# Attention and expert layer on one core: from the tenth turn on, the sums of values and the fifth score chunk in one block

## The chip, the cores and the metric

The kernel runs on one core of one Trainium2 chip. The metric is the time of one execution on the device in microseconds (us), the median of repeated runs. The core has five engines that run side by side, each through its own instructions in a fixed order: TensorE (PE in the profile; its weight loads are PEld), VectorE (DVE), ScalarE (ACT), GpSimd (POOL) and SyncE (SP), which issues the DMAs.

## The reference

Block-causal attention over 8 batches and 8 heads (576 positions, head size 64, blocks of 64), then a two-layer expert network over the 4608 tokens of 512 features, without its bias or routing:

```python
scores = scale * np.matmul(q, k.transpose(0, 1, 3, 2))
mask = block_i >= block_j                      # blocks of 64
scores = np.where(mask, scores, -1000000000.0)
scores = scores - np.max(scores, axis=-1, keepdims=True)
attn = np.exp(scores)
attn = attn / (np.sum(attn, axis=-1, keepdims=True) + 1e-09)
attn = np.matmul(attn, v)
...
h = x @ w_in                                   # 512 -> 2048
g = h * (1.0 / (1.0 + np.exp(-1.702 * h)))
out = g @ w_out                                # 2048 -> 512
```

## The kernel before

**Two pieces of work share the core.** Attention goes in 32 turns n = 0 to 31, one for each pair of heads, and a 33rd that only finishes the last pair. The expert network goes in 12 tiles of 384 tokens, each in 16 slices of 128 hidden features. One slice has 12 products into the PSUM tile `hp` (x and w_in, each split in a high and a low part) and, a slice later, 9 products into three `acc` tiles (g and w_out, split in the same way). `hp` has one buffer. Between the two lies the nonlinearity: ACT computes a tanh from `hp` (L562), DVE makes g from it and `hp` (L563), ACT rounds g to `gh` (L571) and GpSimd computes the rest, `gl` (L82). So the products of slice k+1 into `hp` can't begin before DVE has made g of slice k, and `acc` of slice k comes behind `hp` of slice k+1.

**A turn of attention.** The queries of a head are cut in five chunks, i = 0 to 4; chunk i sees 64(2i+1) keys, so chunk 4 sees all 576. `prep` turns q and k with DVE transposes (L297) into `qk`, the two heads on partitions 0 to 63 and 64 to 127. `score` multiplies, each head on its half of TensorE's rows, so the two heads' products run side by side; a PSUM bank has room for 512 columns, so chunk 4 is cut in 256 and 320 keys and takes four banks. `weigh` masks, scales and takes the maximum on DVE (L351) and the exponential on ACT (L358). `normalise` divides (L368, L371 on DVE) and scales the weights, which `SCALE_ON` gives to an engine: "P" is GpSimd (L376), "D" is DVE (L378). `turn` transposes the weights in 32x32 blocks on DVE (L385, L390; called `turned` in the profile), and behind chunk 4 sixteen DMAs on SP's queue (L397) put these blocks in their places. `av` multiplies them with the values in the next turn, 60 products into two banks, and ACT copies the sums out (L450, L451).

**What sets the order.** `ORDER` writes out the items of a turn: from the tenth turn on (n = 9, since n = 8 has its own string) the third string holds, "3+0/2+1" (the scores of chunks 3, 0, 2, 1), "V" (sums of values of the pair before), "4" (chunk 4), "L" (transposes of the next pair). Between two items `advance` lays expert slices up to a quota from `TILES_BY`, in whole slices. The Tile framework then orders each engine's instructions; code under `high_priority` (the nonlinearity) may move ahead. `bank()` hands out four PSUM banks in rotation in these turns.

Of the kernel before, what the change touches and what calls it, by code (L numbers as in the profile page):

```python
# [10 lines left out]
F32 = mybir.dt.float32  # L11
# [5 lines left out]

SCALE_ON = ("PPPPP", "PPPPP", "PPPPD")  # L20

# [4 lines left out]
ORDER = (  # L26
# [3 lines left out]
)  # L30

START = "1+0 - B 2/3 L C - V - 4 - a - - -"
# [8 lines left out]
def attention_moe_kernel(  # L41
# [9 lines left out]
    nc = tc.nc  # L51
    B, H, S, D = q.shape
    DM, DF = w_in.shape
    P = 128
    BLK = 64
    NDC = DM // P
    NFC = DF // P
    RING = 2 * S
    TT = 384
    TILES = [(t0, min(TT, B * S - t0)) for t0 in range(0, B * S, TT)]  # L60
    NT = len(TILES)
    QC = 4
    NPAIR = B * H // 2
    HP = H // 2
    NCH = 5

    sp = ctx.enter_context(tc.tile_pool(name="sp", bufs=1))
# [6 lines left out]
    def early(n):  # L74

        return n < 2 * HP
# [12 lines left out]
    def bank():  # L89
        tags = ["w0", "w1", "w2"]  # L90
        if not turns["experts"]:
            tags += ["acc0", "acc1", "acc2", "h"]
        elif turns["n"] > 2 * HP:
            tags.append("w3")
        turns["bank"] += 1
        return ps.tile([P, 512], F32, tag=tags[turns["bank"] % len(tags)], name="bank")

    def mm(**kw):
        return tc.keep_in_program_order(nc.tensor.matmul(**kw))  # L99
# [4 lines left out]

    ident = sp.tile([P, P], F32, name="ident")
    make_identity(nc, ident)
    MW = 448
    mask = sp.tile([P, MW], mybir.dt.bfloat16, name="mask")
    nc.gpsimd.memset(mask, 0.0)
    nc.gpsimd.memset(mask[0:BLK, MW - BLK : MW], -8e9)  # L110

# [7 lines left out]
    def room(tag, shape, dt, name):  # L119
        return d2.tile(shape, dt, tag=tag, name=name, bufs=1)  # L120
# [6 lines left out]
        return home[name, g]  # L127

    xr = sp.tile([P, NDC, RING], F32, name="xr")


    vp = sp.tile([P, 2, NCH, D], F32, name="vp")
# [3 lines left out]
    def values(n):  # L136

        if n not in (1, 3):
            return vp
        if n not in vx:  # L140
            vx[n] = room("xl", [P, 2, NCH, D], F32, "vx")
            nc.gpsimd.memset(vx[n][BLK:P, :, NCH - 1, :], 0.0)
        return vx[n]
# [9 lines left out]
    tw, pw = [  # L153
        turned[:, x : x + 4 * NS].rearrange("p (b s) h c -> p b s h c", b=4) for x in (0, 4 * NS - 4)
    ]
# [5 lines left out]
    for i in range(NCH):  # L161
        w, o = BLK * (2 * i + 1), 2 * BLK * i * i
        es.append(flat[:, o : o + 2 * w].rearrange("p (h k) -> p h k", h=2))

    def width(i):
        return BLK * (2 * i + 1)

    def qrange(i):
        return (0, BLK) if i == 0 else (BLK * (2 * i - 1), BLK * (2 * i + 1))
# [6 lines left out]
    for g in range(NG):  # L176
# [3 lines left out]
        for fc in range(FG):  # L180
            r = (g * FG + fc) * P
# [80 lines left out]
    raw, qk = {}, {}  # L262
# [5 lines left out]
    def load(n):  # L268

        if n in (1, 3):  # L270
            raw[n] = room("xh", [P, 2, S // 32, 32], F32, "raw")
        else:
            raw[n] = d2.tile([P, 2, S // 32, 32], F32, tag="raw", name="raw", bufs=1)
        for x, src in enumerate((q, k)):
            queue = nc.scalar if n < 2 and x else nc.sync
            for hd, b, h in heads(n):
                for c in range(0, D, 32):
                    r = hd * D + c
                    queue.dma_start(
                        out=raw[n][r : r + 32, x],  # L280
                        in_=src[b, h][:, c : c + 32].rearrange("(c p) d -> p c d", p=32),
                    )
# [9 lines left out]
    def prep(n):  # L292

        tag = "e0" if early(n) and n % 2 else "qk"
        qk[n] = d2.tile([P, 2, S], F32, tag=tag, name="qk", bufs=1)
        for x in range(2):
            nc.vector.transpose(out=qk[n][:, x], in_=raw[n][:, x].rearrange("p c d -> p (c d)"))  # L297
        raw.pop(n)
        m = follower(n)
        if m is not None:  # L300
            load(m)

    stats = {}

    def score(n, banks):

        if n not in stats:
            mx = d2.tile([P, NCH + 1, 2], F32, tag="mx", name="mx")
            sm = d2.tile([P, NCH, 2], F32, tag="sm", name="sm")
            stats[n] = (mx, sm)  # L310
        todo = []
        for chunks in banks:

            part = []
            for lo, hi in ((0, 512),) if width(chunks[0]) <= 512 else ((0, 256), (256, S)):
                ss = [bank() for _ in range(2)]
                c = 0
                for i in chunks:
                    a, z = qrange(i)
                    w = min(hi, width(i)) - lo  # L320
                    for hd in range(2):
                        r = slice(hd * D, hd * D + D)

                        mm(
                            out=ss[hd][:, c : c + w], lhsT=qk[n][r, 0, a : a + P],
                            rhs=qk[n][r, 1, lo : lo + w], start=True, stop=True,
                        )
                        part.append((i, hd, lo, lo + w, ss[hd][0 : z - a, c : c + w]))
                    c += w
            todo.append(sorted(part, key=lambda x: (chunks[::-1].index(x[0]), x[2])))  # L330
        for chunks, part in zip(banks, todo):
            e = {}
            for i, hd, lo, hi, s in part:
                e[i] = weigh(n, i, hd, lo, hi, s, e.get(i))
            for i in chunks[::-1]:
                normalise(n, i, e[i])
                if not early(n):
                    turn(n, i, e[i])

    def weigh(n, i, hd, lo, hi, s, e):  # L340
# [8 lines left out]
        last = i > 0 and hi == w  # L349
        mk = mask[0:m, MW - (hi - lo) : MW] if last else mask[0:m, 0 : hi - lo]  # L350
        nc.vector.tensor_tensor_reduce(  # L351
# [12 lines left out]
    def normalise(n, i, e):  # L364
# [6 lines left out]
        nc.vector.reciprocal(out=c, in_=c)  # L371
        on = SCALE_ON[phase(n)][i]
        for hd in range(2):
# [52 lines left out]
                in_=src[:, x : x + 2 * len(part), a : a + 2],  # L426
            )

    def av(n):

        b, h = divmod(n, HP)
        before_av(n)
        o, o0 = bank(), bank()

        todo = []
        for i in range(1, NCH):
            c = (i - 1) * P
            todo += [(o, c, P, j, pw[:, :, SLOT[i] + j]) for j in range(i)]
            todo.append((o, c + BLK, BLK, i, pw[:, 2:4, 9 + i]))
        last = len(todo) - 1  # L440
        todo.append((o0, 0, BLK, 0, pw[:, 0:2, 10]))

        for x, (bk, c, nn, j, w) in enumerate(todo):
            for hd in range(2):
                mm(
                    out=bk[hd * D : hd * D + D, c : c + nn].rearrange("d (a c) -> d a c", c=32),
                    lhsT=values(n)[:, hd, j], rhs=w[:, :, hd], start=x in (0, last + 1), stop=x >= last,
                )
        c0 = (b % 2) * S
        nc.scalar.copy(out=xr[:, h, c0 : c0 + BLK], in_=o0[:, 0:BLK])  # L450
        nc.scalar.copy(out=xr[:, h, c0 + BLK : c0 + S], in_=o)  # L451
        m = follower(n)
        if m is not None:
            load_v(m)

    def follower(n):

        m = {0: 2, 1: 3, 2: 4, 3: None}.get(n, n + 1)
        return None if m is None or m >= NPAIR else m

    def order(n):
        return {HP: START, 2 * HP: HANDOVER}.get(n, ORDER[phase(n)]).split()

    def step(n):

        turns["n"] = n
        now = n < NPAIR

        def item(x):
            if x == "V":  # L470
                return (lambda: av(n - 1)) if n else None
            if x == "L":
                return (lambda: prep(n + 1)) if n + 1 < NPAIR else None
            if x in ("a", "B", "C"):
                m, chunks = {"a": (n, [0, 1]), "B": (n - 1, [2, 3]), "C": (n - 1, [4])}[x]
                return (lambda: flip(m, chunks)) if m >= 0 else None
            return (lambda: score(n, [[int(z) for z in y.split("+")] for y in x.split("/")])) if now and x != "-" else None

        return [item(x) for x in order(n)]
# [3 lines left out]
    xs = {}  # L483
# [22 lines left out]
    def chunk_time(tt):  # L506
        return 4 * unit1(tt) + tt // P * 650
# [69 lines left out]
        yield from second(prev)  # L577


    ends = np.cumsum([0.0] + [NFC * chunk_time(tt) for _, tt in TILES])  # L580

    def quota(pos):
        xs, ys = zip(*TILES_BY)
        return -1.0 if pos < xs[0] else np.interp(pos, xs, [ends[y if y >= 0 else y - 1] for y in ys])

    def heads_for(t):
        return -(-sum(TILES[t]) // S) * H
# [36 lines left out]
    for n in range(NPAIR + 1):  # L624
        items = step(n)
        for sl, fn in enumerate(items):
            if fn is not None:
                fn()
            if order(n)[sl] == "V":
                heads_done = 2 * n  # L630
            pos = 2 * (n + (sl + 1) / len(items))
            convert(min(len(pieces), np.interp(pos - 0.5, *zip(*WEIGHTS_BY))))
            lim = quota(pos)
            advance(heads_done, lambda: state["t"] >= lim)
# [30 lines left out]
```

## Time and profile before

| | |
|---|---|
| median of 3 runs (lowest to highest) | 1122.7 us (1121.84 to 1124.51) |
| the profiled execution | 1120.49 us, its span 1118.6 us |
| PE busy | 1076.4 us, 96% of the span |
| PEld busy | 908.7 us, 81% |
| DVE busy | 583.0 us, 52% |
| ACT busy | 498.6 us, 45% |
| POOL busy | 406.7 us, 36% |
| mean granted TensorE clock | 0.992 |

Busy time is the time in which an engine runs at least one instruction; matmuls are pipelined, so consecutive ones overlap in the list and only the distance of their starts tells their cost. "x60" stands for merged instructions of one kind. In the PE rows, "bank" with 60 instructions is the item V, with 16 the item 3+0/2+1, with 8 chunk 4; "hp" with 12 and "acc" with 9 are one slice's halves. A product in full float32 is two matmuls in the profile.

### The profile page before, as it was taken

How to read it: one execution, taken by the hardware profiler on the slowest of the kernel's cores; microseconds unless marked ns; L12 is line 12 of the kernel's file. 1: busy time of each engine (PE TensorE's matmuls, PEld its weight loads, DVE VectorE, ACT ScalarE, POOL GpSimd, SP SyncE). 2: the span in 40 equal slices, each digit the busy share in tenths (PEclk: the TensorE clock that was granted, in tenths of full speed). 3: DMA queues.
4: the chain of work that ended last, by engine and by line, in shares of the span. 5: the costliest groups of instructions: out<-in, count | busy, mean ns of one | idle time of the engine just before them, and what ended most of it. 6: DMA issues, size and time to landing. Idle time of an engine off the chain costs nothing. (4 is left out here: it accounts for less than half of the span.)

```text
span 1118.6 us, 19977 instructions
## 1 busy us (share of the span) xinstructions
PE 1076.4 (96%) x6960; PEld 908.7 (81%) x6960; DVE 583.0 (52%) x1856; ACT 498.6 (45%) x1321; POOL 406.7 (36%) x509
## 2 busy tenths in 40 slices
PE   5969998999999999999999999999999999999998
PEld 3757776788888888888888888888888888899997
DVE  6776885545545555654555655645545654211210
ACT  5866776434534433534443543444434444322322
POOL 4665664333333332333333333333333233122222
PEclk9979999999999999999999999999999999999999
DMA  8734532332444432343443333344342332200000
GB/s 171 205 89 153 150 73 62 84 79 57 105 86 86 103 80 64 64 98 78 98 101 74 75 93 65 70 108 85 81 107 63 71 85 58 54 29 1 29 1 29
DMA packets 219365, 91.25 MB, mean 82 GB/s; under 512 B 197760, under 2 KB 197760, under 8 KB 219264
## 3 DMA queue, kind: packets, MB, share of 16 engines
q1 hardware_dynamic: 214528, 89.38, 34.0%
q10 hardware_dynamic: 4736, 0.59, 0.3%
q8 instruction: 55, 0.90, 0.3%
q14 instruction: 46, 0.38, 0.1%
HBM read 45.09 MB, written 9.44 MB: 49 GB/s over the span
## 5 line engine op out<-in xcount | busy, mean ns | idle before, releaser
L82 POOL TENSOR_TENSOR gl<-g,gh 128x384 fp32r<-128x384 f32 x192 | 194.7, 1014 | 551.5 <-ACT gh L571 449.1
L99 PE MATMUL hp<-xh,wih 128*128 128x384 f32 x768 | 264.7, 345 | 7.9 <-DVE g L563 6.9
L563 DVE SCALAR_TENSOR_TENSOR g<-g,hp 128x384 f32<-128x384 f32 x192 | 105.9, 552 | 319.1 <-ACT g L562 317.8
L99 PE MATMUL hp<-xh,wil 128*128 128x384 f32 x768 | 258.4, 336 | 0.1
L562 ACT ACTIVATE g<-hp 128x384 f32<-128x384 f32 x192 | 94.1, 490 | 359.8 <-PE hp L99 354.8
L99 PE MATMUL hp<-xl,wih 128*128 128x384 f32 x768 | 253.9, 338 | 0.4 <-DVE xl L82 0.4
L99 PE MATMUL acc<-woh,gh 128*128 128x512 f32 x576 | 233.9, 406 | 0.0
L99 PE MATMUL acc<-wol,gh 128*128 128x512 f32 x576 | 226.9, 394 | 0.0
L99 PEld LDWEIGHTS hp<-xh,wih 128*128 128x128 f32 x768 | 144.2, 188 | 34.1 <-DVE g L563 23.1
L99 PE MATMUL acc<-woh,gl 128*128 128x512 f32 x576 | 167.9, 393 | 0.3 <-POOL gl L82 0.3
L571 ACT CAST gh<-g 128x384 fp32r<-128x384 f32 x192 | 98.4, 513 | 156.5 <-DVE g L563 156.4
L99 PEld LDWEIGHTS hp<-xh,wil 128*128 128x128 f32 x768 | 144.3, 188 | 6.5 <-POOL wil L82 0.7
L358 ACT ACTIVATE e<-e,mx 64x64 f32<-64x64 f32 (+4 forms) x240 | 132.3, 552 | 37.6 <-DVE mx L351 37.6
L376 POOL TENSOR_TENSOR e<-e,sm 64x64 f32<-64x64 f32 (+1 forms) x192 | 113.6, 612 | 95.0 <-DVE sm L371 46.5
L99 PEld LDWEIGHTS hp<-xl,wih 128*128 128x128 f32 x768 | 143.6, 188 | 1.3 <-DVE xl L82 1.3
L99 PE MATMUL bank<-qk 64*128 64x320 f32 (+4 forms) x768 | 122.5, 428 | 14.5 <-DVE qk L297 11.1
L99 PEld LDWEIGHTS acc<-woh,gh 128*128 128x128 f32 x576 | 107.9, 187 | 34.2 <-issue 10.5
L99 PEld LDWEIGHTS acc<-woh,gl 128*128 128x128 f32 x576 | 107.8, 188 | 25.9 <-POOL gl L82 1.2
L99 PEld LDWEIGHTS acc<-wol,gh 128*128 128x128 f32 x576 | 108.3, 188 | 16.7 <-POOL wol L82 0.3
L351 DVE CUSTOM_DVE_ANT_0 e<-bank,mask 64x64 f32<-64x64 f32 (+4 forms) x240 | 89.7, 417 | 56.9 <-PE bank L99 52.8
L385 DVE STREAM_TRANSPOSE turned<-e 128x384 f32<-128x384 f32 (+1 forms) x192 | 92.3, 499 | 48.8 <-POOL e L376 48.3
L99 PEld LDWEIGHTS bank<-qk 64*128 64x128 f32 x768 | 69.6, 193 | 54.2 <-issue 25.4
(50 smaller groups left out, 956.0 us busy)
## 6 DMA issues: line engine op xcount, KB each, us to landing
turned<-turned SPq DMA_DIRECT2D x192, 80.0 KB, 2.1
turned<-turned SPq DMA_DIRECT2D x96, 112.0 KB, 2.2
raw<-in_q_dram SPq DMA_DIRECT2D x128, 72.0 KB, 2.4
out_dram<-osb SPq DMA_DIRECT2D x36, 256.0 KB, 2.2
raw<-in_k_dram SPq DMA_DIRECT2D x120, 72.0 KB, 2.6
turned<-turned SPq DMA_DIRECT2D x96, 88.0 KB, 2.1
words<-in_moe_w_in_dram SPq DMA_DIRECT2D x16, 512.0 KB, 6.3
vp<-in_v_dram SPq DMA_DIRECT2D x60, 128.0 KB, 2.4
```

Source lines behind the costliest of these rows:

```text
L82: eng.tensor_tensor(out=out, in0=in0, in1=in1, op=ALU.subtract)
L99: return tc.keep_in_program_order(nc.tensor.matmul(**kw))
L351: nc.vector.tensor_tensor_reduce(out=e[0:m, hd, lo:hi], in0=s, in1=mk, op0=ALU.add, op1=ALU.min, scale=-0.125, scalar=3e38 if lo == 0 else ...
L358: nc.scalar.activation(out=e[0:m, hd], in_=e[0:m, hd], func=AF.Exp, scale=-1.0, bias=mx[0:m, i, hd : hd + 1], accum_out=sm[0:m, i, hd : hd ...
L376: nc.gpsimd.tensor_tensor(out=x, in0=x, in1=sc.to_broadcast([m, width(i)]), op=ALU.mult)
L385: nc.vector.transpose(out=tw[:, :, SLOT[i] : SLOT[i] + i, hd].rearrange("p b j c -> p j b c"), in_=e[:, hd, 0 : i * P],)
L562: nc.scalar.activation(out=g, in_=hp[:, 0:tt], func=AF.Tanh, scale=1.702)
L563: nc.vector.scalar_tensor_tensor(out=g, in0=g, scalar=1.0, in1=hp[:, 0:tt], op0=ALU.add, op1=ALU.mult)
L571: nc.scalar.copy(out=gh, in_=g)
```

## The change

From n = 9 on, the items "V" and "4" become one item "V4", laid directly one behind the other. `av` gets its small bank `o0` from outside and writes it first; chunk 4's scores of the first 512 keys go to one bank for each head, and the scores of the last 64 keys of both heads go into columns 64 to 191 of `o0` by one product. For that product `prep` writes the last 64 keys of the two heads into `ends`, a tile of 128 partitions with zeros where a head's rows meet the other head's columns, so that all 128 rows of both heads' queries give both results. The item L moves from the end of the string two places forward. GpSimd scales chunk 4 in these turns (SCALE_ON). In all turns, `av` now does the product into `o0` first, and no longer last. A variable of the planner is renamed.

```diff
-SCALE_ON = ("PPPPP", "PPPPP", "PPPPD")
+SCALE_ON = ("PPPPP", "PPPPP", "PPPPP")
...
-    "3+0/2+1 - - - V - - 4 - - - L -",
+    "3+0/2+1 - - - - V4 - - - L - -",
...
-    MW = 448
+    MW = 576
...
+    ends = sp.tile([P, 2, BLK], F32, name="ends")
+    nc.gpsimd.memset(ends, 0.0)
...
-            nc.vector.transpose(out=qk[n][:, x], in_=raw[n][:, x].rearrange("p c d -> p (c d)"))
+            z = QC * P if x and n > 2 * HP else S
+            nc.vector.transpose(out=qk[n][:, x, 0:z], in_=raw[n][:, x, 0 : z // 32].rearrange("p c d -> p (c d)"))
+            for hd in range(2 if z < S else 0):
+                r = slice(hd * D, hd * D + D)
+                nc.vector.transpose(
+                    out=ends[r, hd], in_=raw[n][r, x, z // 32 : S // 32].rearrange("p c d -> p (c d)")
+                )
...
-            for lo, hi in ((0, 512),) if width(chunks[0]) <= 512 else ((0, 256), (256, S)):
+            cuts = (0, 512) if width(chunks[0]) <= 512 or shared is not None else (0, 256, S)
+            for lo, hi in zip(cuts, cuts[1:]):
...
+            if shared is not None:
+                i = NCH - 1
+                mm(
+                    out=shared, lhsT=qk[n][:, 0, slice(*qrange(i))], rhs=ends.rearrange("p h k -> p (h k)"),
+                    start=True, stop=True,
+                )
+                part += [(i, hd, QC * P, S, shared[:, hd * BLK : (hd + 1) * BLK]) for hd in range(2)]
...
-    def av(n):
+    def av(n, o0=None):
...
-        todo.append((o0, 0, BLK, 0, pw[:, 0:2, 10]))
+        todo.insert(0, (o0, 0, BLK, 0, pw[:, 0:2, 10]))
...
+    def values_and_4(n):
+        o0 = bank()
+        av(n - 1, o0)
+        if n < NPAIR:
+            score(n, [[NCH - 1]], o0[:, BLK : 3 * BLK])
...
+            if x == "V4":
+                return lambda: values_and_4(n)
```

Three places of the programs, one turn in the middle of the run. In the names, `g_7154<-g_7154,hp_7141` is g made from that `hp`. The first place is PE, from the last sums of values on. Before:

```order
L99 MATMUL bank_7143<-turned_75,vp_73 64x64 x2
L99 MATMUL acc0_6759<-woh_894,gh_7107 128x512
...
L99 MATMUL hp_7189<-xh_977,wih_1123 128x384
...
L99 MATMUL acc0_6759<-woh_894,gh_7136 128x512
...
L99 MATMUL hp_7218<-xh_977,wih_1123 128x384
...
L99 MATMUL bank_7238<-qk_6983 128x256
L99 MATMUL bank_7239<-qk_6983 128x256
L99 MATMUL bank_7242<-qk_6983 128x320
L99 MATMUL bank_7243<-qk_6983 128x320
L99 MATMUL acc0_6759<-woh_1335,gh_7203 128x512
```

Two slices stood between V and chunk 4. After, on PE at the same place:

```order
L99 MATMUL bank_7162<-turned_77,vp_75 64x64 x2
L99 MATMUL bank_7199<-qk_6971 128x512
L99 MATMUL bank_7200<-qk_6971 128x512
L99 MATMUL bank_7161<-ends_73,qk_6971 128x128
L99 MATMUL acc0_6750<-woh_896,gh_7126 128x512
...
L99 MATMUL hp_7243<-xh_979,wih_1125 128x384
...
L99 MATMUL acc0_6750<-woh_1337,gh_7155 128x512
...
L99 MATMUL hp_7272<-xh_979,wih_1125 128x384
```

Chunk 4 now stands right behind V, and the two slices stand behind it. The second place is DVE, from behind chunk 2's weights on. Before:

```order
L390 STREAM_TRANSPOSE turned_75<-e_7065 64x2x2x32
L563 SCALAR_TENSOR_TENSOR g_7202<-g_7202,hp_7189 128x384
L351 ISA e_7246,mx_7024<-bank_7238,mask_69 128x256
...
L563 SCALAR_TENSOR_TENSOR g_7231<-g_7231,hp_7218 128x384
L351 ISA e_7246,mx_7024<-bank_7239,mask_69 128x256
...
L297 STREAM_TRANSPOSE qk_7305<-raw_6986 128x576 x2
L368 TENSOR_SCALAR sm_7025<-sm_7025 128x2
L371 RECIPROCAL sm_7025<-sm_7025 128x2
L378 TENSOR_SCALAR e_7246<-e_7246,sm_7025 128x576 x2
L385 STREAM_TRANSPOSE turned_75<-e_7246 128x4x4x32 x2
L390 STREAM_TRANSPOSE turned_75<-e_7246 64x2x2x32
L563 SCALAR_TENSOR_TENSOR g_7298<-g_7298,hp_7285 128x384
```

After, on DVE from the g of the `hp` just ahead of V:

```order
L591 SCALAR_TENSOR_TENSOR g_7154<-g_7154,hp_7141 128x384
L403 STREAM_TRANSPOSE turned_77<-e_7033 128x3x4x32 x2
L369 ISA e_7050,mx_7014<-bank_7022,mask_69 128x192
...
L408 STREAM_TRANSPOSE turned_77<-e_7055 64x2x2x32
L369 ISA e_7204,mx_7014<-bank_7199,mask_69 128x512
...
L302 STREAM_TRANSPOSE qk_7292<-raw_6976 128x576
L386 TENSOR_SCALAR sm_7015<-sm_7015 128x2
L389 RECIPROCAL sm_7015<-sm_7015 128x2
L403 STREAM_TRANSPOSE turned_77<-e_7204 128x4x4x32 x2
L408 STREAM_TRANSPOSE turned_77<-e_7204 64x2x2x32
L591 SCALAR_TENSOR_TENSOR g_7256<-g_7256,hp_7243 128x384
```

The two g that stood between the work on chunks 1, 2 and that on chunk 4 are gone from there: DVE now does both lots of attention work between two g. The third place is GpSimd (after):

```order
L82 TENSOR_TENSOR gl_7156<-g_7154,gh_7155 128x384
L394 TENSOR_TENSOR e_7050<-e_7050,sm_7015 128x192 x2
L394 TENSOR_TENSOR e_7055<-e_7055,sm_7015 128x320 x2
L394 TENSOR_TENSOR e_7204<-e_7204,sm_7015 128x576 x2
L82 TENSOR_TENSOR gl_7258<-g_7256,gh_7257 128x384
```

The scaling of chunk 4 (128x576, twice) is new there, between two `gl`.

More of the change, by code (lines that the diff above doesn't have):

```diff
@@ L303, in attention_moe_kernel, with score @@
     stats = {}
-    def score(n, banks):
+    def score(n, banks, shared=None):
         if n not in stats:
@@ L427, in flip @@
             )
-    def av(n):
+    def av(n, o0=None):
         b, h = divmod(n, HP)
         before_av(n)
-        o, o0 = bank(), bank()
+        o = bank()
+        if o0 is None:
+            o0 = bank()
         todo = []
@@ L446, in av @@
                     out=bk[hd * D : hd * D + D, c : c + nn].rearrange("d (a c) -> d a c", c=32),
-                    lhsT=values(n)[:, hd, j], rhs=w[:, :, hd], start=x in (0, last + 1), stop=x >= last,
+                    lhsT=values(n)[:, hd, j], rhs=w[:, :, hd], start=x in (0, 1), stop=x in (0, last),
                 )
@@ L459, in follower @@
         return None if m is None or m >= NPAIR else m
+    def values_and_4(n):
+        o0 = bank()
+        av(n - 1, o0)
+        if n < NPAIR:
+            score(n, [[NCH - 1]], o0[:, BLK : 3 * BLK])
     def order(n):
@@ L577, in moe @@
         yield from second(prev)
-    ends = np.cumsum([0.0] + [NFC * chunk_time(tt) for _, tt in TILES])
+    tile_ends = np.cumsum([0.0] + [NFC * chunk_time(tt) for _, tt in TILES])
     def quota(pos):
         xs, ys = zip(*TILES_BY)
-        return -1.0 if pos < xs[0] else np.interp(pos, xs, [ends[y if y >= 0 else y - 1] for y in ys])
+        return -1.0 if pos < xs[0] else np.interp(pos, xs, [tile_ends[y if y >= 0 else y - 1] for y in ys])
     def heads_for(t):
@@ L628, in attention_moe_kernel @@
                 fn()
-            if order(n)[sl] == "V":
+            if order(n)[sl][0] == "V":
                 heads_done = 2 * n
```

## The prediction

> **What bounds the kernel.** I read the page first, then the chain that ended last, then the timelines of PE and DVE in one turn. The page, its span and first group of rows:
>
> ```profile
> span 1118.6 us, 19977 instructions
> PE 1076.4 (96%) x6960; PEld 908.7 (81%) x6960; DVE 583.0 (52%) x1856; ACT 498.6 (45%) x1321; POOL 406.7 (36%) x509
> ```
>
> TensorE is nearly always at work. So a change gains if it takes columns or boundaries from PE, and loses if it makes PE wait. The chain that ended last, one turn of it (start, length, engine):
>
> ```profile
> 870.22 2.92 PE bank L99 x60
> 873.13 2.26 PE acc L99 x9
> ...
> 879.58 2.26 PE hp L99 x12
> 881.84 1.17 PE bank L99 x8
> 883.01 2.27 PE acc L99 x9
> ...
> 889.47 2.36 PE hp L99 x12
> 891.83 2.04 PE bank L99 x16
> 893.87 2.24 PE acc L99 x9
> 896.11 2.10 PE hp L99 x12
> 898.21 2.08 PE acc L99 x9
> ...
> 902.40 2.92 PE bank L99 x60
> ```
>
> The chain is PE alone. A slice away from attention takes 2.10 + 2.08 = 4.18 us; next to an attention block its halves take 2.26 or 2.27, so a boundary costs some 0.16 to 0.19 on a side. A turn is 902.40 - 870.22 = 32.18 us: 6 slices (25.08), blocks of 2.92, 1.17 and 2.04, and 0.97 for boundaries and waits.
>
> How close DVE is to this chain is seen where only one slice stood between V and chunk 4. The rows of PE, then of DVE, in such a turn:
>
> ```profile
> 262.95 2.99 PE L99 MATMUL bank<-turned,vp 128*64 128x128 f32 x60
> 270.23 1.24 PE L99 MATMUL bank<-qk 64*128 64x256 f32 x8
> 278.78 0.45 PE L99 MATMUL hp<-xh,wih 128*128 128x384 f32 x1 [0.85 <-DVE g L563]
> ```
>
> ```profile
> 263.63 0.56 DVE L563 SCALAR_TENSOR_TENSOR g<-g,hp 128x384 f32<-128x384 f32 x1 [3.64 <-ACT g L562]
> 264.11 1.03 DVE L385 STREAM_TRANSPOSE turned<-e 128x384 f32<-128x384 f32 x2
> 265.28 0.36 DVE L351 CUSTOM_DVE_ANT_0 e<-bank,mask 128x192 f32<-128x192 f32 x1
> 266.90 0.17 DVE L371 RECIPROCAL sm<-sm 128x2 f32<-128x2 f32 x1
> 271.32 0.31 DVE L390 STREAM_TRANSPOSE turned<-e 64x128 f32<-64x128 f32 x1
> 271.77 0.43 DVE L351 CUSTOM_DVE_ANT_0 e<-bank,mask 128x256 f32<-128x256 f32 x1
> 273.87 1.44 DVE L297 STREAM_TRANSPOSE qk<-raw 128x576 f32<-128x576 f32 x2
> 275.24 0.17 DVE L368 TENSOR_SCALAR sm<-sm 128x2 f32<-128x2 f32 x1
> 276.51 1.30 DVE L385 STREAM_TRANSPOSE turned<-e 128x512 f32<-128x512 f32 x2
> 278.17 0.55 DVE L563 SCALAR_TENSOR_TENSOR g<-g,hp 128x384 f32<-128x384 f32 x1
> ```
>
> DVE works in order. From the g at 263.63 it does chunk 3's transposes, all of chunks 1 and 2 until 271.63, then all of chunk 4, and only then, at 278.17, the g that frees `hp`; PE waited for it, 0.85 us, though from V's start it had V, chunk 4 and five slice halves to do before it.
>
> **The change, part by part.**
>
> *The products of chunk 4.* By the two blocks of scores (2.04 us for 1024 columns of a head, 1.17 for 576) a column costs 0.87/448 = 1.94 ns. Two heads side by side over 512 columns: 0.18 less than 576, or 1.05. The shared product has 128 columns, nothing beside it: 0.25. Together 1.30, which is 0.13 more than before.
>
> *The boundary.* One block less in a turn: 0.16 ahead of chunk 4 and 0.19 behind it go. The step from V's form of the array (128 rows by 64) to the scores' (64 by 128), and from there to the full one, is new and not in any such row; between 0 (the slice behind pays it anyway) and 0.35 (all of it comes back). I take 0.12, since a side costs 0.16 to 0.19 and includes filling. The sum on PE alone is 0.13 - 0.35 + 0.12 = -0.10 a turn, in 23 turns -2 us (bounds -5 and +3).
>
> *Waits that go.* Waits of `hp` for DVE, from the list of waits:
>
> ```profile
> PEld hp L99 <- DVE g L563: 23.1, 41, 2.0
> ```
>
> These contain the ordinary gap of each; not all are in these turns. I take 0.3 a turn (2.36 against 2.10 in the row of 889.47) and 0.85 more in six turns of the kind of 278.78: 7 + 5 = -12 us (bounds 0 and -20).
>
> *Two transposes more in `prep`, the zeroing of `ends`, the wider mask, the order inside `av`:* DVE has 48% idle and these lie behind the g that matters or ahead of the loop: 0. If DVE is the bound for a stretch, the two small transposes stand behind that g in most turns.
>
> *The new wait.* This is the large term. By the order above, DVE now does chunks 1, 2 and chunk 4 between the g of the slice ahead of V and the g of the first slice behind chunk 4, and the second `hp` behind chunk 4 waits for the latter. PE's cover from V's start is V 2.92, 0.1, chunk 4 1.30, `acc` 2.27, `hp` 2.10, `acc` 2.09: 10.8 us. DVE from V's start (262.95 in the rows): g at 0.68, chunk 3 at 1.16, the scores of chunk 1 at 2.33, the last transpose of chunk 2 done at 8.68. That part doesn't change. Then chunk 4, with these rows for the pieces (groups with shapes kept apart, then ACT in the same turn):
>
> ```profile
> L376 POOL TENSOR_TENSOR turned<-turned,sm 128x576 f32<-128x576 f32 x16 | 18.0, 1146 | 5.7 <-DVE sm L371 2.6 <-DVE mx L351 2.0 <-ACT xr L450 0.8
> L351 DVE CUSTOM_DVE_ANT_0 e<-bank,mask 128x448 f32<-128x448 f32 x48 | 27.7, 610 | 0.0
> 273.58 0.78 ACT L358 ACTIVATE e<-e,mx 128x576 f32<-128x576 f32 x1 [0.36 <-DVE mx L351]
> 274.35 0.77 ACT L358 ACTIVATE e<-e,mx 128x576 f32<-128x576 f32 x1
> 267.24 0.97 POOL L376 TENSOR_TENSOR e<-e,sm 128x192 f32<-128x192 f32 x2 [1.42 <-ACT e L358]
> ```
>
> Two of 512 at about 0.6 (610 ns for 448, pipelined) and two of 64 make 1.5; the first exponential begins at 1.47, and from there to the sum's instruction are 275.24 - 273.58 = 1.66: 3.13; the reciprocal 0.2 later; GpSimd 0.34 after that (267.24 - 266.90): 3.67; twice 1.146: 5.96; the second transpose 0.65 and the small one 0.31: 7.0; g 0.55: 7.55. So `hp` may begin at 8.68 + 7.55 + 0.06 = 16.3 after V's start: a wait of 5.5 us. DVE's own two scalings (0.95) are gone, but it now waits 2.3 for GpSimd's. (The PE gap also has a part ahead of chunk 4, whose banks are those of chunks 1 and 2; that is the same wait, moved.)
>
> The order lists differ from turn to turn in where that g stands. In 8 of the 23 turns it stands as shown: 5.5 each. In 5 it stands between chunk 4's two transposes, 1.5 earlier: 4.0. In 5 it stands ahead of them and chunk 3's transposes ahead of the g before V: 7.5 + 4.2 = 11.75, a wait of 1.0. In 2 only the first of these holds: 2.7. In one, chunk 1's and 2's scores are read ahead of V: 2.9. In 2 a new tile's split lies in between: I take 3. The sum is 44 + 20 + 5 + 5.4 + 2.9 + 6 = 83 us. Bounds by the pieces that no row has (512 columns, the 64 columns, GpSimd's start): 1 us a turn either way, 60 and 106.
>
> *GpSimd.* Its 46 scalings (53 us) stand ahead of the `gl` of the g that is late anyhow; that `gl` is wanted only 2.1 + 1.4 us after. No cost beyond the above. *SP's queue:* the sixteen DMAs behind chunk 4 start some 2 us later after its products than before, but the V that needs them now follows a whole turn later and not 20.6 us (881.84 to 902.40): 0.
>
> *The clock.* Idle PE has a price of its own, in three windows of the trace (length, then busy time of PE, PEld, DVE, ACT and POOL, granted clock, DMA):
>
> ```profile
> 15.50:19.00 3.50, 3.43 (x19) 2.58 (x19) 2.25 (x13) 2.73 (x10) 3.19 (x5) 0.57 0.74 135
> 55.00:59.90 4.90, 2.38 (x30) 1.87 (x24) 4.40 (x9) 2.25 (x6) 4.04 (x5) 1.00 0.04 6
> 59.90:73.50 13.60, 9.68 (x42) 6.51 (x42) 10.93 (x35) 11.17 (x34) 7.22 (x10) 0.52 0.70 180
> ```
>
> After a stretch with PE half idle the granted clock was 0.52 for 13.6 us; near the start it was 0.57 for only 3.5, a loss of 3.5 x 0.43 = 1.5 us. A wait of 5.5, of which 4.8 stand in one piece, is more idle than that stretch had; one of 1.0 is not. I take four short halvings, 1.5 us each: +6 (0 to 35, one in every turn). The Trainium skill, "TensorE: Matmul & The Clock Gate", Part 1, says that the clock halves after about 3.4 us of an idle window that runs freely, and returns after as much work. By that rule, as an estimate from that page, a wait of 4.8 us would hold a whole window in some 4 of 10 cases, and the shorter ones seldom; the trace agrees in direction, though its long halving came where PE was not wholly idle.
>
> **The sum** is made against the profiled execution, 1120.5 us, which lies 2.2 below the median: 1120.5 - 2 - 12 + 83 + 6 = 1195.5, and with the 2.2, 1198.
>
> **Rivals.** First, faster: DVE keeps up. It decides at 10.8 us from V's start to the freed `hp`; then no wait is new, the old ones go, and the time is 1122.7 - 14 = 1109. For it speaks that with two slices between (row 881.84) DVE lost only 0.3; against it that the same work lost 0.85 with a cover 4 us longer. 5%. Second, a short wait: about 1 us a turn, if exponentials and GpSimd run further ahead than I think: 1109 + 23 = 1132. 8%. Third, the clock halves in nearly every turn: 1198 - 6 + 35 = 1227, and more if a halving outlasts 3.4 us. 13%. Fourth, the gain on PE and the waits cancel, within 0.2% of the time before (about what a measurement of this kernel can tell from no change): 2%.
>
> **Numbers.** The main case has 72%, its own range 1169 to 1230 (83 taken as 60 to 106, and the clock's 0 to 15). To hold 8 in 10 it must reach the third rival's time and its margin: 1158 to 1245. Faster by over 0.2%: 5%. Within it: 2%. Slower: 93%.
>
> **What the profile after would show.** Right: a list of waits in which `hp` waits for g (L591) with some 80 us and a longest of 5 to 6; turns of 33 to 38 us; PE busy down to about 91%; chunk 4's block 1.3 us long directly behind V; the two scalings of GpSimd between chunk 4's exponentials and its transposes, and DVE idle there. Wrong: `hp` waits below 30 us in all, or turns all below 32.2. I would be wrong most easily if the scores of chunks 1 and 2 were read earlier than behind the g ahead of V.

## The result, and the profile after

| | before | after |
|---|---|---|
| median (lowest to highest, 4 runs each, same chip) | 1122.27 us (1120.21 to 1124.51) | 1238.53 us (1238.06 to 1243.09) |
| ratio | | 1.1045 [1.1011, 1.1078] |
| span of the profiled execution | 1118.6 us | 1236.3 us |
| mean granted TensorE clock | 0.992 | 0.960 |

The change costs 116 us. The page after, its span and first group of rows, and the granted clock in 40 slices:

```profile
span 1236.3 us, 20043 instructions
...
PE 1111.7 (90%) x6914; PEld 942.1 (76%) x6914; DVE 577.1 (47%) x1854; ACT 494.9 (40%) x1321; POOL 460.6 (37%) x558
...
PEclk8979998999899998999899899999999989999999
```

PE runs fewer matmuls than before (6914 against 6960) and is yet busy 35 us longer: the digits 8 in the clock, spread over the turns, say why. VectorE is no busier than before. So the loss is not work. From the list of waits, with the engine and tile that waits, the engine and tile waited for, us in all, times, longest:

```profile
PEld hp L99 <- DVE g L591: 89.5, 26, 5.6
...
PE hp L99 <- DVE g L591: 78.2, 26, 5.2
...
PEld bank L99 <- DVE mx L369: 19.6, 26, 4.6
...
PE bank L99 <- DVE mx L369: 15.3, 20, 4.3
```

Before, the row of PEld waiting for g had 23.1 us and a longest of 2.0. That of PE itself, without the ordinary gap of a weight load, and that of PE waiting for a bank were:

```profile
PE hp L99 <- DVE g L563: 6.9, 7, 1.8
...
PE bank L99 <- DVE mx L351: 3.4, 5, 1.5
```

One turn after, as the timeline has it, first PE (start, us, instruction, in brackets the idle time ahead of it and what ended it):

```profile
755.77 2.98 PE L99 MATMUL bank<-turned,vp 128*64 128x64 f32 x60
759.50 1.53 PE L99 MATMUL bank<-qk 64*128 64x512 f32 x4 [0.75 <-DVE mx L369]
760.97 0.49 PE L99 MATMUL bank<-ends,qk 128*128 128x128 f32 x2
761.21 0.47 PE L99 MATMUL acc<-woh,gh 128*128 128x512 f32 x1
...
772.61 0.69 PE L99 MATMUL hp<-xh,wih 128*128 128x384 f32 x1 [4.90 <-DVE g L591]
```

Then DVE in the same turn, from the g ahead of chunk 3's transposes to the g that PE waits for:

```profile
756.75 0.55 DVE L591 SCALAR_TENSOR_TENSOR g<-g,hp 128x384 f32<-128x384 f32 x1 [3.93 <-ACT g L590]
...
758.95 0.48 DVE L369 CUSTOM_DVE_ANT_0 e<-bank,mask 128x320 f32<-128x320 f32 x1
759.36 0.08 DVE L369 DVE_READ_ACCUMULATOR2_ANT mx<- 128x1 f32 x1
...
764.40 0.31 DVE L408 STREAM_TRANSPOSE turned<-e 64x128 f32<-64x128 f32 x1
764.85 0.69 DVE L369 CUSTOM_DVE_ANT_0 e<-bank,mask 128x512 f32<-128x512 f32 x1
...
769.82 0.71 DVE L403 STREAM_TRANSPOSE turned<-e 128x512 f32<-128x512 f32 x1 [1.32 <-POOL e L394]
770.92 0.71 DVE L403 STREAM_TRANSPOSE turned<-e 128x512 f32<-128x512 f32 x1 [0.39 <-POOL e L394]
771.66 0.31 DVE L408 STREAM_TRANSPOSE turned<-e 64x128 f32<-64x128 f32 x1
772.00 0.55 DVE L591 SCALAR_TENSOR_TENSOR g<-g,hp 128x384 f32<-128x384 f32 x1
```

Chunks 1 and 2 are done at 764.71, 8.94 us after V's start (the prediction had 8.68; in seven of the eight longest turns it is 8.65 to 8.68). Chunk 4 and the g take from there to 772.55, 7.8 us (7.55). `hp` starts 16.84 us after V (16.3; in six of the eight it is 16.55 to 16.58), and PE had 5.1 us nothing to do. Single waits for a g are told here and below, unless a row is named, as the distance between the starts of the products on both sides beyond the usual 0.23 us; that is some 0.16 more than the bracket. The same turn in windows, with the length, the busy times of PE, PEld, DVE, ACT and POOL, then the granted clock, DMA share and GB/s:

```profile
767.00:772.00 5.00, 0.71 (x4) 0.23 (x2) 2.33 (x6) 1.47 (x5) 2.25 (x2) 1.00 0.00 0
772.00:776.20 4.20, 3.59 (x12) 3.59 (x13) 1.54 (x4) 0.51 (x1) 1.01 (x1) 0.59 0.54 129
```

Behind the wait the clock is at 0.59: from the first product of `hp` at 772.61 to the block behind it, at 776.33, are 3.72 us, and 2.10 otherwise. The wait is paid for a second time.

### The profile page after: what moved, and what is told of

Same layout as the page of the kernel before. It is cut to its first block, busy times and chain, and to the rows that moved or that the text cites. A ratio compares the mean times of both kernels' runs of the same rounds, so it can differ in the third digit from the quotient of the medians.

```text
span 1236.3 us, 20043 instructions
## 1 busy us (share of the span) xinstructions
PE 1111.7 (90%) x6914; PEld 942.1 (76%) x6914; DVE 577.1 (47%) x1854; ACT 494.9 (40%) x1321; POOL 460.6 (37%) x558
## 4 chain that ended last, share of the span: by engine, by line
PE 54%; DVE 10%; ACT 6%; POOL 6%; issue 6%; DMA 1%; DVEq 0%; POOLq 0%; SPq 0%; ACTq 0%
PE hp L99 27%; PE acc L99 22%; POOL e L394 6%; ACT e L376 5%; PE bank L99 5%; DVE turned L403 3%; DVE e L369 2%; DVE g L591 2%; DVE turned L408 1%; ACT g L590 1%; DVE sm L386 1%; DVE sm L389 1%; DMA out_dram<-osb 1%; ACT gh L599 0%; DVE mx L369 0%
## 5 line engine op out<-in xcount | busy, mean ns | idle before, releaser
L99 PE MATMUL hp<-xh,wih 128*128 128x384 f32 x768 | 273.7, 356 | 78.2 <-DVE g L591 78.2
L99 PE MATMUL hp<-xh,wil 128*128 128x384 f32 x768 | 267.8, 349 | 1.3 <-POOL wil L82 1.3
L99 PE MATMUL hp<-xl,wih 128*128 128x384 f32 x768 | 263.2, 350 | 0.4 <-DVE xl L82 0.4
L394 POOL TENSOR_TENSOR e<-e,sm 64x64 f32<-64x64 f32 (+4 forms) x240 | 167.8, 720 | 192.5 <-DVE sm L389 149.1
L99 PEld LDWEIGHTS hp<-xh,wih 128*128 128x128 f32 x768 | 151.6, 197 | 100.9 <-DVE g L591 89.5
L99 PEld LDWEIGHTS hp<-xh,wil 128*128 128x128 f32 x768 | 151.6, 197 | 8.8 <-POOL wil L82 2.1
L99 PEld LDWEIGHTS hp<-xl,wih 128*128 128x128 f32 x768 | 150.7, 197 | 1.2 <-DVE xl L82 1.2
L99 PE MATMUL bank<-qk 64*128 64x320 f32 (+5 forms) x676 | 125.9, 456 | 19.6 <-DVE mx L369 11.0
L99 PEld LDWEIGHTS bank<-qk 64*128 64x128 f32 x676 | 65.2, 194 | 56.8 <-issue 21.8
L369 DVE CUSTOM_DVE_ANT_0 e<-bank,mask 64x64 f32<-64x64 f32 (+5 forms) x240 | 100.4, 468 | 12.4 <-PE bank L99 6.5
```

Of the source, the lines that this page charges most:

```text
L369: nc.vector.tensor_tensor_reduce(out=e[0:m, hd, lo:hi], in0=s, in1=mk, op0=ALU.add, op1=ALU.min, scale=-0.125, scalar=3e38 if lo == 0 else ...
L394: nc.gpsimd.tensor_tensor(out=x, in0=x, in1=sc.to_broadcast([m, width(i)]), op=ALU.mult)
```

## The experiments

All times are medians; each ratio is against runs of the kernel before on the same chip. The before of these runs stood at 1123.0 to 1123.9 us.

**1. GpSimd's part.** The kernel after, with chunk 4's scaling back on DVE:

```diff
-SCALE_ON = ("PPPPP", "PPPPP", "PPPPP")
+SCALE_ON = ("PPPPP", "PPPPP", "PPPPD")
```

> The changed kernel with one part undone: VectorE scales chunk 4 again, all else as changed. Theory A (VectorE does chunks 1, 2 and 4 between two g, whoever scales): from the reciprocal on, 0.95 of scaling and two transposes in place of 0.34 + 2.29 of GpSimd and the second transpose, and the list puts g one or two instructions earlier; the long waits of hp fall from 5.1 to some 3.8, the middle ones from 3.5 to 2.3, the sum from 81 to about 56, fewer halvings of the clock; 1200 to 1212. Theory B (GpSimd's scaling is what makes VectorE late): no waits beyond those of the kernel before, 1110 to 1125.

Measured: 1221.13 us, 1.0868 [1.0853, 1.0883]. The row of waits:

```profile
PEld hp L99 <- DVE g L591: 73.1, 26, 4.2
```

The waits fall by 16 us and the time by 17. The scaling on GpSimd is a part of the loss, a seventh, and not its cause. The gain is less than expected: the waits were to fall by 25 us, and those that are left are still followed by a slow clock, in 13 stretches of half clock in the turns, 47.8 us, against 15 and 68.3 us after the whole change.

**2. The order inside `av`, taken back for the early turns.** After, with the product into `o0` last again wherever chunk 4 doesn't share the bank:

```diff
-        todo.insert(0, (o0, 0, BLK, 0, pw[:, 0:2, 10]))
...
+        if joined:
+            todo.insert(0, first)
...
+        else:
+            todo.append(first)
...
```

> The changed kernel, but in the turns before the tenth the product into the small bank of the sums of values is the last again, as before the change; from the tenth turn on it is first, as changed. In the changed trace the ninth scores block of four chunks already begins 9.5 us late, and 4.3 of it is one wait of the sums of values for the bank that chunks 1 and 2 still hold. Theory A (the order inside the sums costs it): 4 to 9.5 us come back, 1229 to 1234. Theory B (the early loss is the free-running clock window and would come with any change of the program): within 2 us of 1238.

Measured: 1228.47 us, 1.0931 [1.0915, 1.0947]; 10 us off the time, a little more than expected. The row of PE waiting for a bank falls from 15.3 (longest 4.3) to 11.2 (longest 1.5).

**3. GpSimd's part alone.** The kernel before, with chunk 4 scaled on GpSimd:

```diff
-SCALE_ON = ("PPPPP", "PPPPP", "PPPPD")
+SCALE_ON = ("PPPPP", "PPPPP", "PPPPP")
```

> The kernel before with one part of the change alone: GpSimd scales chunk 4 from the ninth turn on, V and chunk 4 stay two slices apart. Theory A (waits add up along VectorE's list between two g): the g behind chunk 4 comes 1.0 us later (0.34 + 2.29 + 0.05 + 0.65 + 0.31 against 0.95 + 1.30 + 0.31), in every turn 0.8 to 1.0 more wait, 1140 to 1147. Theory C (one block instead of two is the whole cause, GpSimd costs nothing where a slice lies in between): 1120 to 1125.

Measured: 1145.3 us, 1.0204 [1.0187, 1.022].

```profile
PEld hp L99 <- DVE g L563: 44.6, 41, 2.2
```

As often as before (41), and twice as long. No stretch of half clock in the turns: waits of up to 2 us bring none here.

**4. The order inside `av` alone.** The kernel before, with the product into `o0` first in all turns:

```diff
+        todo.insert(0, (o0, 0, BLK, 0, pw[:, 0:2, 10]))
...
-        todo.append((o0, 0, BLK, 0, pw[:, 0:2, 10]))
...
```

> The kernel before with one part of the change alone: in all turns the product into the small bank is the first of the sums of values. Theory A (it asks for a bank that VectorE has not yet read): 4 to 10 us slower by turns up to the ninth, 1126 to 1132; more if in later turns the bank of chunks 1 and 2 is asked for too. Theory B (no effect, the early loss is the clock): 1121 to 1124.

Measured: 1133.33 us, 1.0088 [1.0072, 1.0104]: 10 us for an edit that I had costed at nothing. The largest single place is V of the turn n = 8. Its row in the kernel after the change, then the corresponding one before:

```profile
204.83 5.14 PE L99 MATMUL bank<-turned,vp 128*64 128x64 f32 x60 [4.32 <-DVE mx L369]
```

```profile
195.05 2.87 PE L99 MATMUL bank<-turned,vp 128*64 128x128 f32 x56
```

The rotation gives `o0` the bank that scores of chunks 1 and 2 hold until DVE has read them. Before, 56 of the 60 matmuls go ahead (V is 30 products of two matmuls each), and only the last four meet that bank. With `o0` first, all 60 wait behind it. In this experiment's own trace the wait there is 4.31 us, and V then takes 5.15 us at half clock; before, the last four waited 1.52 us. That is about half of the 10 us. The other half is lost in the turns ahead: the V ahead of it already starts at 174.30, and at 169.28 before. One wait of this kind is seen at 56.85, 2.00 us for copies of ACT (L411); the rest I have not followed.

**5. Why the chunks are read so late.** Chunks 1 and 3 share a buffer for their weights (`e1`), so DVE may not read chunk 1's scores, nor those behind them, before chunk 3 is transposed. After, with a buffer of its own for chunk 1:

```diff
-e = d2.tile([P, 2, w], F32, tag=f"e{i % 2}", name="e", bufs=1)
+e = d2.tile([P, 2, w], F32, tag="wm" if i == 1 else f"e{i % 2}", name="e", bufs=1)
```

> The changed kernel, with one thing added: from the ninth turn on chunk 1's weights have a buffer of their own (that of the merged expert weights, free by then) and no longer chunk 3's. Then VectorE reads the scores of chunks 1 and 2 long before V, and between the two g in question stand six transposes (2.6 us) and chunk 4, not 8.0 us and chunk 4. GpSimd still scales chunk 4, and V and chunk 4 are still one block. Theory A (the length of VectorE's list between the two g): from V's start 3.8 to 4.05 for the first scores of chunk 4, and 7.55 to the end of g: 11.6 against the 10.6 that PE has; waits of 0.5 to 1.1 a turn, no halving of the clock, 1130 to 1142 (10 of it from the turns before the tenth). Theory B (GpSimd's scaling or the joined block as such): over 1180.

Measured: 1162.66 us, 1.034 [1.0326, 1.0354]; 76 of the 116 us go with one buffer.

```profile
PEld hp L99 <- DVE g L591: 57.1, 41, 2.9
```

The longest wait falls from 5.6 to 2.9 us, and the half clock in the turns from 68.3 us to a single stretch of 3.4. The size was missed by 21 to 33 us: about 1.2 us of wait stays in most turns, 1.7 to 2.7 in some.

**6. The same buffer in the kernel before,** the same edit.

> The kernel before, with the same buffer of its own for chunk 1's weights. Theory A: of 10 us of waits of hp for g and some 4 us of refilling behind them, those behind V and those in the six turns with one slice between V and chunk 4 go (about 1 us in each of the six); 0.17 a turn behind chunk 4 stays: 6 to 9 us faster, 1113 to 1118. Rival: these waits are covered elsewhere, 1121 to 1124.

Measured: 1127.59 us, 1.004 [1.0022, 1.0058]. Missed on both theories: steady turns fall from 32.2 to 32.0 us, but four of the early ones, where one slice stands between V and chunk 4, rise from 32.9 to between 34.8 and 36.0. In the first of these four PE waits 2.50 us (in the bracket) at 262.69 for a g ahead of the next V, which on DVE now stands behind the reading of chunks 1 and 2. So the buffer is no gain by itself; what it is worth in the kernel after is the repair of what joining broke.

**7. Joining alone.** The kernel before, with V and chunk 4 adjacent, but with four banks of its own for chunk 4, no shared product, and DVE scaling:

```diff
-    "3+0/2+1 - - - V - - 4 - - - L -",
+    "3+0/2+1 - - - - V 4 - - - L - -",
```

> The kernel before with one thing changed: V and chunk 4 stand directly one behind the other, with L moved as in the change, but without the shared bank and product, and VectorE scales chunk 4. Theory A (joining them puts both lots of VectorE's work between two g, whatever banks and products they use): waits as in the changed kernel with VectorE's scaling, 2.4 to 3.7 us in most turns and a dozen halvings, 1195 to 1214. Theory D (the shared bank, held until the last 64 keys are read, or the third product does the harm): 1120 to 1135.

Measured: 1186.85 us, 1.0553 [1.0538, 1.0568].

```profile
PEld hp L99 <- DVE g L563: 41.4, 26, 3.4
...
PEld bank L99 <- ACT xr L451: 23.5, 19, 1.3
...
PEld bank L99 <- DVE mx L351: 14.4, 24, 1.7
```

The new place alone, with L moved as in the change, costs 63 us, more than any other part. It came out some 8 us below my range. A part of the time goes to waits for banks ahead of chunk 4 here (V's sums not copied out, scores not read); while PE waits there it can't be waiting for g, which I had not taken off. The edits of experiments 3, 4 and 7, each alone, cost 22, 10 and 63 us, 95 of the 116. The rest goes with the shared bank and product, or with how the parts act together; sharing was not run alone, so its own cost is open.

**8. All three repairs together** in the joined kernel, the edits of experiments 1, 2 and 5:

```diff
+SCALE_ON = ("PPPPP", "PPPPP", "PPPPD")
...
+        if joined:
+            todo.insert(0, first)
...
+        else:
+            todo.append(first)
...
+e = d2.tile([P, 2, w], F32, tag="wm" if i == 1 else f"e{i % 2}", name="e", bufs=1)
```

> The changed kernel with all three costs taken away: chunk 1's own buffer, VectorE scaling chunk 4, and the small bank's product last before the tenth turn. Theory A: from V's start 4.05 for the first scores, 3.5 to the reciprocal, 0.95 scaling, 1.3 transposes, 0.55 g: 10.4 against PE's 10.6, so no wait, the 14 us of waits of the kernel before are gone and so is one block boundary a turn (1.3 in all): 1107 to 1114, the fastest of all. If it stays above 1120, something of the joined block is not understood.

Measured: 1127.42 us, 1.003 [1.0017, 1.0042]: 111 of the 116 us are back, and no gain. 13 of 23 turns have no long wait, and eleven of these take 31.7 to 31.9 us, less than the 32.2 before; but the ten others have a wait of 1.7 to 2.7 us. In one of them, DVE:

```profile
809.32 0.30 DVE L386 TENSOR_SCALAR sm<-sm 128x2 f32<-128x2 f32 x1 [0.84 <-ACT e L376]
809.66 0.17 DVE L389 RECIPROCAL sm<-sm 128x2 f32<-128x2 f32 x1
809.86 0.51 DVE L408 STREAM_TRANSPOSE turned<-e 64x128 f32<-64x128 f32 x2
811.40 0.31 DVE L408 STREAM_TRANSPOSE turned<-e 64x128 f32<-64x128 f32 x1 [1.03 <-POOL e L394]
811.74 0.56 DVE L598 SCALAR_TENSOR_TENSOR g<-g,hp 128x384 f32<-128x384 f32 x1
```

It is the same mechanism at another g: this one stands behind chunk 2's small transpose, which waits 1.03 us for GpSimd's scaling of chunk 2.

**9 and 10. Chunk 2, then chunks 1 and 2, scaled on DVE,** in the kernel of experiment 8:

```diff
-SCALE_ON = ("PPPPP", "PPPPP", "PPPPD")
+SCALE_ON = ("PPPPP", "PPPPP", "PPDPD")   # 9
+SCALE_ON = ("PPPPP", "PPPPP", "PDDPD")   # 10
```

> The repaired joined version, and in these turns DVE scales chunk 2 as well, so that the small transposes behind chunk 2 no longer stand behind GpSimd. Theory A (the waits of 1.7 to 2.7 us that were left in ten turns came from DVE standing idle for GpSimd's scaling of chunk 2, 1.0 us, and from the g queued behind it): in the turns where that g stands behind the small transposes its wait falls by 0.7 to 1.5 us; the waits between hp and acc fall from 19 us to 8 to 13 us, and the time is 1116 to 1122 us. Rival B (DVE's own work, not its waiting, is the length of that stretch): the two scalings, 0.3 us each, take back what the waiting cost; 1125 to 1130.

> As the run with chunk 2 on DVE, with chunk 1 on DVE too: no transpose of these chunks waits for GpSimd. Theory A (waiting for GpSimd decides): as good as the other or better, 1113 to 1121 us. Rival B (DVE's work decides): 0.2 us of scaling twice a turn on DVE ahead of the same g makes it slower than the other by 2 to 6 us; 1120 to 1132.

Measured: 1119.18 us, 0.9967 [0.9955, 0.9978], and 1121.68 us, 0.9983 [0.9972, 0.9993]. With chunk 2 on DVE the waits of PEld for g fall from 27.3 to 19.0 us, and the joined kernel is faster than the one before, by 4 us. Chunk 1 on DVE brings nothing more and costs 2.5 us: a few turns of 31.7 or 31.9 rise to 32.4 or 32.6, as rival B had it.

**11 and 12. The same without joining.** The kernel before with chunk 2 on DVE as its only edit, and with chunk 1's buffer besides:

```diff
-SCALE_ON = ("PPPPP", "PPPPP", "PPPPD")
+SCALE_ON = ("PPPPP", "PPPPP", "PPDPD")   # 11 and 12
...
+e = d2.tile([P, 2, w], F32, tag="wm" if i == 1 else f"e{i % 2}", name="e", bufs=1)   # 12
```

> The kernel before with one edit: in the turns from the tenth on DVE scales chunk 2 too. Theory A (what the repaired joined version gains over the kernel before is PE's shorter turn, 31.7 against 32.2 us, from the joined block): without joining the edit brings next to nothing, since only waits of some 0.2 us a turn are there to go; 1119 to 1125 us, and turns of 32.0 to 32.3. Rival B (the gain is the scaling's alone and joining adds nothing): 1117 us or below, turns of 31.7 or less.

> The kernel before with chunk 1's own buffer and DVE scaling chunk 2, without joining. Theory A (joining is worth about 0.3 us a turn once its waits are gone): 1118 to 1124 us, that is slower than the joined version with the same two edits (1119) by 0 to 5 us; its steady turns 31.9 to 32.1, and the four early turns of 34.8 to 36.0 that the buffer alone had fall to about 33.5. Rival B (joining is worth nothing even repaired): 1112 to 1118.

Measured: 1115.01 us, 0.992 [0.9906, 0.9933], the best of all kernels here, and 1123.26 us, 0.9996 [0.9987, 1.0005]. In experiment 11 my theory A falls: one letter of SCALE_ON is worth 9 us without joining. Rival B's time came, but not its turns of 31.7 us or less. PEld's waits for g:

```profile
PEld hp L99 <- DVE g L563: 12.7, 24, 2.0
```

Nearly half of the 23.1 us before is gone. The place is the one that the prediction showed, one slice between V and chunk 4. Chunk 2 on DVE before:

```profile
270.18 0.45 DVE L385 STREAM_TRANSPOSE turned<-e 128x256 f32<-128x256 f32 x1 [0.90 <-POOL e L376]
270.86 0.45 DVE L385 STREAM_TRANSPOSE turned<-e 128x256 f32<-128x256 f32 x1 [0.23 <-POOL e L376]
```

And in experiment 11:

```profile
265.36 0.56 DVE L563 SCALAR_TENSOR_TENSOR g<-g,hp 128x384 f32<-128x384 f32 x1 [3.64 <-ACT g L562]
...
271.05 0.68 DVE L378 TENSOR_SCALAR e<-e,sm 128x320 f32<-128x320 f32 x2
...
279.24 0.56 DVE L563 SCALAR_TENSOR_TENSOR g<-g,hp 128x384 f32<-128x384 f32 x1
```

DVE stood idle 1.13 us for GpSimd; doing the scaling itself takes 0.68. From the first g to the last it now needs 279.24 - 265.36 = 13.88 us instead of 14.54, and such turns fall from 32.9 to 32.2 us, the steady ones from 32.2 to 32.0. Experiment 12 came out as A had it: with the same two edits joining is worth 4 us (1119.18 against 1123.26), but the buffer costs more than that, 8 us (1123.26 against 1115.01). The joined kernel with chunk 2 on DVE and without the buffer was not run; whether it would stand below 1115 is open.

## Why the prediction was right, and where its terms were off

The sign, the place and the mechanism were right. The size was not: 1238.5 is 40 us above the number given and above the range of the main case (1169 to 1230). It lies in the full range (1158 to 1245) because that was stretched for the third rival, the slow clock in nearly every turn, and the clock makes only some 14 of the 40 us. So the number fell inside in part by luck. Term by term:

*PE alone, -2.* Chunk 4's block takes 1.47 + 0.24 from 759.50 to 761.21 in the row above, and 1.06 + 0.24 = 1.30 where its banks are free, as predicted. (Of the working, "0.18 less than 576" is wrong: 64 columns at 1.94 ns are 0.12. The 1.05 that the sum uses is right.) The later gain of joining, 4 us in experiments 9 and 12, is of the size of this term's lower bound (-5). It may come from it and from the wait of 0.26 us behind chunk 4 that goes; that was not tested apart.

*The new wait, 83, with 12 of old ones gone.* The mechanism was right, the size some 15 us short: 71 predicted on balance, 86 measured. The row of PE's waits for g rises from 6.9 to 78.2 us, by 71, and ahead of and inside chunk 4's block PE waits besides for the banks of chunks 1 and 2, 0.94 us in 13 turns and some 1.2 in two, 15 us in all (in the turn above 0.75 ahead of the block, most of the rest inside it). The prediction counted these as a part of its waits. With them, eight turns wait 6.0 to 6.3 us (5.5 predicted), five 4.4 to 4.7 (4.0), and four that have no wait for a bank 1.4 (1.0). So each turn is 0.4 us or more longer than foreseen. In the eight longest, two sizes were off: DVE lets `hp` begin 16.55 us after V or later, and not 16.3, because chunk 4 with its g takes some 7.8 us and not 7.55; and PE has 10.6 us of work in that time without the waits for banks, and not 10.8. That DVE's order decides, and not GpSimd's speed, is what experiments 1, 5 and 7 show.

*"That is the same wait, moved": 0.* By the trace this held. DVE is through with chunks 1 and 2 as foreseen (8.65 to 8.68 us after V), and it reads chunk 4's scores long after they are there (764.85 against 761.21 above). So the g comes at the same time whether PE waits for the banks or not, and what PE waits there it doesn't wait for the g. No run has these banks free and all else as it is.

*The order inside `av`, 0.* This step failed: 10 us, by experiments 2 and 4 alike. I had looked at it as work of DVE. It is one product of PE that was put ahead of 56 matmuls on an engine that works them off in order, and at n = 8 the bank it needs was the last to come free. The turns before the tenth were in the diff ("in all turns") and not in my sum.

*The clock, 6 (four halvings).* The mechanism was right, the size off by a factor of three: 15 stretches, 68.3 us at half clock in the turns, about 20 us of time (the distances between `hp`'s products exceed the ordinary by 23.0 us in these turns, before by some 4). That lies halfway between my 6 and the third rival's 35. The number of long waits was right, 13 foreseen and 14 found; wrong was that I let four of them halve the clock, and all did.

The four parts, 71 and 15 for the waits, 10 for the order and 20 for the clock, make 116 of the 117.7 us between the two spans; the last two are rounded, so the match is closer than the parts are known.

*What was to be seen.* Waits of 80 us with a longest of 5 to 6, PE at about 91% (90%), chunk 4 directly behind V and DVE idle during GpSimd's scaling all came. Turns of 33 to 38 us became 32.6 to 40.6, since the longest have the slow clock as well.

The rival "faster" (DVE keeps up below 10.8 us) had its condition far off: the freed `hp` comes 16.55 to 16.85 us after V in the eight longest turns and 12.0 in the shortest. Even with all repairs, joining made it only to 1119.

## What to carry to other kernels

Where one engine works in order for two streams, count what it does between two releases of a buffer with a single copy, against the work that the waiting engine has in hand; joining two blocks on the busy engine takes the cover away from between them, and may cost many times what a boundary costs. A short operation handed to another engine isn't free if the giver's next instruction needs its result: here 0.68 us done by itself was better than 1.13 us of waiting. And a product put first in a block takes its bank's wait for the whole block.

## What the hardware showed that I had not expected

A wait need not be long to halve the clock. After the change all 14 waits from 3.45 to 5.3 us, and one of 2.0, were followed by `hp` blocks of 2.8 to 4.0 us instead of 2.1; the half-clock stretches are 3.41 us or a multiple. In experiment 1 so were all eight waits from 3.6 to 4.0 us, and five of nine from 2.4 to 2.8, as in these windows around one of 2.4:

```profile
434.00:436.30 2.30, 0.23 (x1) 0.00 (x0) 1.60 (x5) 0.97 (x3) 0.00 (x0) 1.00 0.00 0
436.30:440.00 3.70, 3.50 (x13) 3.51 (x14) 1.90 (x5) 0.51 (x1) 1.02 (x1) 0.64 0.21 51
```

The Trainium skill, "TensorE: Matmul & The Clock Gate", Part 1, puts the halving behind at least one idle window of about 3.4 us. The length of the stretches agrees. That a window must be idle as a whole does not: a wait of 3.5 us would then hold one in about 1 case of 40 (0.09 of 3.41), and all six were followed by a slow clock.

What goes with the half clock here is how busy PE was in one window of a fixed grid. In each trace all half-clock stretches start whole multiples of 3.41 us apart, so the grid is known. Two of its windows, the first with a half-clock stretch right behind it, the second with none:

```profile
253.72:257.13 3.41, 1.58 (x8) 1.10 (x7) 1.21 (x7) 2.52 (x6) 1.23 (x2) 1.00 0.00 0
509.72:513.13 3.41, 1.60 (x7) 0.94 (x6) 2.91 (x9) 3.15 (x8) 0.00 (x0) 1.00 0.00 0
```

Over the turns of all 14 traces, all 46 windows at full clock with PE busy for 1.55 us or less (45%) were followed by half clock. Between 1.55 and 1.60 one was and one was not. Of those with 1.60 or more only four of some 3600 were, all in experiment 7, with 2.07 to 2.18; why these four, I can't tell from the traces. By these figures a wait of 2 to 3 us halves the clock when some 1.85 us of idle time fall into one window, and doesn't when the grid cuts it into shorter parts. For a sum of this kind I would now take every wait over 3.4 us as paid again with some 1.5 us, and one of 2.4 to 3 us in about half of the cases.
